# A causal convolution regrouped into 32-token blocks on two column tiles, inside a fused attention and convolution kernel

## The chip, the cores and the metric

One core of one Trainium2 chip. The metric is the device time of one execution in microseconds (us); lower is better. Each timing below is a median over executions in one series, and the kernel before was run again in every series on the same chip. Runs carry a state; verdicts and ratios use fast runs alone, and a verdict of faster or slower asks for 2%. The granted clock is the share of its full clock that TensorE had; the clock records of these traces know 1.0 and 0.5 alone, called full and half clock below. A ratio is the mean time of one kernel's fast runs over that of the other's fast runs of the same rounds, so it is not quite the ratio of the medians quoted beside it.

## The reference, cut to what matters

One layer mixes two branches by a gate per token: attention with 16 heads that share one key and value head, and a causal convolution along the sequence whose kernel K comes from a state space model. S = 2048 tokens, D = 448 channels, 256 states.

```python
g = sigmoid((x * gate_w).sum(-1))
# a: 16 query heads of 28, one key head, one value head
p = softmax((q @ k.T) * 28**-0.5);  a = (p @ v) @ wo
# b: K[d, l] = Re sum_n C[d,n] * exp(dt[d] * A[d,n] * l) * dt[d] * B[d,n]
b = causal_convolution(x, K) + x * Dskip
out = g * a + (1 - g) * b
```

The exponentials of the softmax (16 x 2048 x 2048) are the work of ScalarE, VectorE builds the tables from which TensorE makes K, and TensorE does everything else: scores (QK), attention times values (PV), the kernel generator, the convolution, the projections.

## The kernel before

The program is a list of operations with a modelled price in ns and a priority. A small scheduler, which runs when the kernel is built, orders them on each engine; the order is then fixed. The convolution works channel by channel: for a channel, T holds kernel values in a form made for matrix products, and U holds the inputs. Four channels (j) run beside each other on four column tiles, strips of 32 columns of TensorE's array that `tile_position` names.

```python
def conv(self, c):                       # a chunk of 16 channels
    for k in range(4):
        self.tload(gi)                   # T: 1 MB from device memory for 4 channels
        for m in range(1, 16, 2):
            for j in range(4):
                e.matmul(ps.v(32*j, 33-m, po + 128*k, [[1, 128]]),             # out
                         self.U.v(0, P, (m-1)*D + 4*gi + j, [[D, 33-m]]),      # weights
                         self.T.v(0, P, s*4096 + (960 - 64*m)*4 + j, [[4, 128]]),  # streamed: step of 4 elements
                         start=(m == 1), stop=(m == 15), tile_position=(0, 32*j))
            pg.op("pe", mm, 112, ..., mode="c32")       # price 112 ns for the group of four
    # ... one VectorE operation scales and flips the chunk; then ytr() transposes on TensorE and adds into O

def qk(b):                               # scores of 2 or 3 tiles of 128 x 512, then one exponential over them
    e.matmul(self.psS..., kT.v(32*h, DH+1, ...), qT..., tile_position=(32*h, 0))
    e.activation(expT..., self.psS.v(0, P, 1536*s, [[1, n]]), AF.Exp, scale=SQ)

def pv(st):                              # four heads on four column tiles, summed in psB over 16 steps
    e.matmul(self.psB.v(32*h, 32, 0, [[1, 512]]), vaug..., expT..., start=(kt == 0), stop=(kt == 15), tile_position=(0, 32*h))
```

The four channels of a T load are interleaved, element by element. Elements are bf16, so a step of 4 elements is 8 bytes.

## Time and profile before

| kernel before | value |
|---|---|
| time, median of 3 runs | 540.65 us (538.36 to 541.66) |
| span of the profiled run | 537.2 us |
| mean granted TensorE clock | 0.921 |
| busy share PE, DVE, ACT | 90%, 90%, 91% |
| exponentials: busy, idle time just before them | 470.8 us, 19.0 us |

The span is made of four parts that add up: a start, the exponentials' busy time, the gaps between them, and the tail from the last exponential to the end. With the last exponential ending at 519.5 us this is 29.7 + 470.8 + 19.0 + 17.7 = 537.2 us. "Start" here is that end less busy time less gaps. The profile lines behind it stand in the prediction.

### The profile page before, as it was taken

Reading aid. Unit: us, or ns where it says so; the run is one execution under the profiler, and the core shown is the slowest. Engines: PE = TensorE matmul, PEld = TensorE weight load, DVE = VectorE, ACT = ScalarE, POOL = GpSimd, SP = SyncE. Lnnn points to the kernel's source line nnn. Section 1 sums busy time; section 2 is a strip of 40 time slices with the busy share of each in tenths; the row PEclk is TensorE's granted clock in tenths of the full one; section 3 lists DMA queues with packets and bytes.
Section 4 is the critical chain, followed back from the end, with each engine's and each line's share of the span. In section 5 each row is a group of like instructions: output and inputs, shape, how many; then the busy total and the mean of one; then the engine's idle time right before and its main releaser. Section 6 shows DMA issues by size and latency. Waiting matters only on the chain.

```text
span 537.2 us, 18418 instructions
## 1 busy us (share of the span) xinstructions
PE 484.8 (90%) x8229; PEld 243.8 (45%) x8229; DVE 483.9 (90%) x1168; ACT 487.5 (91%) x428; POOL 4.9 (1%) x17
## 2 busy tenths in 40 slices
PE   6778888999999899999999999999999998998893
PEld 5411132553545444554545445554455543544452
DVE  4978899998999999999999999999999999999023
ACT  4599998998999999999999999999999999999960
POOL 3000000000000000000000000000000000000000
PEclk9855566997999999999999999999999999889997
DMA  8735445777798867779898896778877796697954
GB/s 232 145 79 137 138 139 207 245 285 299 249 327 297 303 230 237 253 265 345 304 337 320 262 332 238 242 260 319 309 296 267 285 393 220 176 388 254 350 188 137
DMA packets 42266, 138.16 MB, mean 257 GB/s; under 512 B 8168, under 2 KB 24476, under 8 KB 27852
## 3 DMA queue, kind: packets, MB, share of 16 engines
q1 hardware_dynamic: 40396, 135.71, 73.7%
q10 hardware_dynamic: 1792, 1.29, 0.8%
q8 instruction: 64, 1.05, 0.8%
q14 instruction: 14, 0.11, 0.1%
HBM read 133.01 MB, written 3.85 MB: 255 GB/s over the span
## 4 chain that ended last, share of the span: by engine, by line
PE 47%; ACT 36%; DVE 12%; DMA 2%; issue 1%; POOL 1%; DVEq 0%; POOLq 0%
ACT expT L977 35%; PE psS L967 13%; PE psS L853 12%; PE psB L985 8%; PE psX L792 6%; PE psX L676 2%; DMA T<-KP_scratch 2%; DVE tab L767 2%; DVE tmp L762 2%; DVE tab L759 2%; PE psS L504 1%; PE psX L877 1%; PE psX L831 1%; DVE O L883 1%; DVE tab L776 1%
## 5 line engine op out<-in xcount | busy, mean ns | idle before, releaser
L977 ACT ACTIVATE expT<-psS 128x1536 bf16<-128x1536 f32 (+1 forms) x410 | 470.8, 1254 | 19.0 <-PE psB L985 12.9
L967 PE MATMUL psS<-qT,kT 29*128 29x512 bf16 x1024 | 170.6, 412 | 29.6 <-ACT expT L977 27.2
L853 PE MATMUL psS<-T,U 128*26 128x128 bf16 (+7 forms) x3584 | 157.9, 303 | 0.6 <-DMA T<-KP_scratch 0.5
L853 PEld LDWEIGHTS psS<-T,U 128*26 128x26 bf16 (+7 forms) x3584 | 113.9, 152 | 35.3 <-issue 28.2
L985 PE MATMUL psB<-expT,vaug 128*32 128x512 bf16 x1024 | 108.8, 417 | 1.4 <-ACT gtok L643 1.3
L967 PEld LDWEIGHTS psS<-qT,kT 29*128 29x128 bf16 x1024 | 39.6, 92 | 124.4 <-ACT expT L977 92.8
L762 DVE TENSOR_TENSOR tmp<-tab,mbf 128x2048 bf16<-128x2048 bf16 (+4 forms) x140 | 78.0, 563 | 0.0
L759 DVE TENSOR_TENSOR tab<-tab,mbf 128x2048 bf16<-128x2048 bf16 (+4 forms) x140 | 77.9, 563 | 0.0
L767 DVE TENSOR_TENSOR tab<-tab,tmp 128x2048 bf16<-128x2048 bf16 (+4 forms) x140 | 77.8, 563 | 0.0
L792 PE MATMUL psX<-tab 128*32 128x96 bf16 x1792 | 54.8, 268 | 1.3 <-issue 1.2
L985 PEld LDWEIGHTS psB<-expT,vaug 128*32 128x32 bf16 x1024 | 26.6, 95 | 64.2 <-issue 60.8
L792 PEld LDWEIGHTS psX<-tab 128*32 128x32 bf16 x1792 | 41.2, 116 | 14.2 <-issue 9.0
L776 DVE TENSOR_TENSOR tab<-tab,mbf 128x2048 bf16<-128x2048 bf16 x28 | 34.0, 1216 | 0.0
L778 DVE TENSOR_TENSOR tab<-tab,mbf 128x2048 bf16<-128x2048 bf16 x28 | 34.0, 1213 | 0.0
L861 DVE TENSOR_TENSOR cst<-psS,omq 128x512 bf16<-128x512 f32 x28 | 19.0, 680 | 15.7 <-PE psS L853 15.5
L717 DVE TENSOR_TENSOR msq<-mst 128x256 f32<-128x256 f32 x63 | 26.2, 416 | 0.0
L676 PE MATMUL psX<-xT,Wq 112*128 112x512 bf16 x64 | 21.7, 436 | 0.4 <-DVE O L838 0.2
L727 DVE CAST mbf<-mst 128x256 bf16<-128x256 f32 x70 | 20.1, 288 | 0.1
L720 DVE TENSOR_TENSOR mst<-msq 128x128 f32<-128x128 f32 x70 | 19.7, 282 | 0.0
L723 DVE SCALAR_TENSOR_TENSOR mst<-mst 128x128 f32<-128x128 f32 x63 | 17.8, 283 | 0.0
L804 DVE TENSOR_REDUCE kstg<-psX 128x128 bf16<-128x256 f32 x28 | 11.7, 418 | 4.2 <-PE psX L792 4.1
L730 DVE TENSOR_SCALAR mbf<-mst 128x128 bf16<-128x128 f32 x70 | 15.3, 218 | 0.0
(112 smaller groups left out, 255.8 us busy)
## 6 DMA issues: line engine op xcount, KB each, us to landing
T<-KP_scratch SPq DMA_DIRECT2D x112, 1024.0 KB, 7.8
rdenB<-R_scratch SPq DMA_DIRECT2D x60, 64.0 KB, 3.8
U<-in_A_x_dram SPq DMA_DIRECT2D x3, 896.0 KB, 5.4
tab<-in_A_x_dram SPq DMA_DIRECT2D x4, 448.0 KB, 6.9
O<-Z_scratch SPq DMA_DIRECT2D x1, 1792.0 KB, 13.6
KP_scratch<-kstg SPq DMA_DIRECT2D x28, 64.0 KB
xT<-in_A_x_dram SPq DMA_DIRECT2D x1, 1792.0 KB, 9.2
U<-Z_scratch SPq DMA_DIRECT2D x1, 896.0 KB, 8.0
```

Source lines behind the costliest of these rows:

```text
L676: pg.op("pe", lambda e, T=T: e.matmul(px, self.Wq.v(0, DT, T * 512 + g * 128, [[1, 128]]), self.xT.v(0, DT, T * S + 512 * qc, [[1, 512]]), ...
L717: pg.op("dve", lambda e, k=k: e.tensor_tensor(msq.v(0, P, 0, [[1, 2 * BW]]) if k > 1 else msq.v(0, P, 0, [[BW, 2], [1, BW]]), src_both(k - ...
L759: pg.op("dve", lambda e, d=dst, a=src, ra=ra, w=w: e.tensor_tensor(d, a, mbf.v(0, P, ra, [[8, 16], [0, 2 * w], [1, 4]]), ALU.mult), el(n, ...
L762: pg.op("dve", lambda e, a=src, rb=rb, w=w: e.tensor_tensor(tmp.v(0, P, so, [[4 * w, 32], [1, 4 * w]]), a, mbf.v(0, P, rb, [[4, 32], [0, w ...
L767: pg.op("dve", lambda e, d=dst, t=t2: e.tensor_tensor(d, d, t, ALU.add), el(n, 1.92), rd=[("tmp", s), ("tab", s, lv + 1)], wr=[("tab", s, ...
L776: pg.op("dve", lambda e: e.tensor_tensor(ua, src, mbf.v(0, P, ra, [[8, 8], [0, 64], [1, 4]]), ALU.mult), el(2048, 1.92), rd=rk + mk, wr=[( ...
L778: pg.op("dve", lambda e: e.tensor_tensor(ub, src, mbf.v(0, P, rb, [[4, 16], [0, 32], [1, 4]]), ALU.mult), el(2048, 1.92), rd=rk + mk, wr=[ ...
L792: r = e.matmul(self.psX.v(32 * g, 32, 96 * jj, [[1, 96]]), tab.v(0, P, o + 768, [[4, 32]]), tab.v(0, P, o, [[256, 3], [4, 32]]), start=(co ...
L853: r = e.matmul(ps.v(32 * j, 33 - m, po + 128 * k, [[1, 128]]), self.U.v(0, P, (m - 1) * D + 4 * gi + j, [[D, 33 - m]]), self.T.v(0, P, s * ...
L967: r = e.matmul(self.psS.v(0, P, 1536 * s + 512 * k, [[1, 512]]), kT.v(32 * h, DH + 1, 128 * kt, [[1, 128]]), qT.v(32 * h, DH + 1, 512 * qs ...
L977: pg.op("act", lambda e: e.activation(expT.v(0, P, 512 * (i0 % 10), [[1, n]]), self.psS.v(0, P, 1536 * s, [[1, n]]), AF.Exp, scale=SQ), 75 ...
L985: r = e.matmul(self.psB.v(32 * h, 32, 0, [[1, 512]]), vaug.v(0, P, 32 * kt, [[1, 32]]), expT.v(0, P, 512 * ((4 * st + h) % 10), [[1, 512]] ...
```

## The change

The intent: each convolution matmul streams 64 columns instead of 128, T takes 112 loads of 512 KB in place of 1024 KB, and the flip of the results moves from a VectorE access pattern to two small TensorE matmuls with a reversal matrix J. The stacking over lag quarters gives the weights up to 64 columns, so two column tiles replace four. U is contiguous in time. The diff cut to its core:

```diff
-            for m in range(1, 16, 2):
-                def mm(e, k=k, m=m, s=s, gi=gi):
-                    for j in range(4):
-                        r = e.matmul(ps.v(32 * j, 33 - m, po + 128 * k, [[1, 128]]),
-                                     self.U.v(0, P, (m - 1) * D + 4 * gi + j, [[D, 33 - m]]),
-                                     self.T.v(0, P, s * 4096 + (960 - 64 * m) * 4 + j, [[4, 128]]),
-                                     start=(m == 1), stop=(m == 15), tile_position=(0, 32 * j), ...)
-                pg.op("pe", mm, 112, ..., mode="c32")
+            for k1 in range(2):
+                for mg in range(2):
+                        for m in range(8 * mg, 8 * mg + 8, 2):
+                            for par in range(2):
+                                r = e.matmul(ps.v(64 * par, 64 - m, po + 64 * pr, [[1, 64]]),
+                                             self.U.v(0, P, uo + (32 * par + e0 + pr) * UC + m, [[1, 64 - m]]),
+                                             self.T.v(0, P, s * self.TW + (448 - 32 * m) * 4 + 2 * k1 + par, [[4, 64]]),
+                                             start=(m == 0), stop=(m == 14), tile_position=(0, 64 * par), ...)
+                    pg.op("pe", mm, 118, ..., mode="c64")     # price 118 ns for the group of eight
...
+    def jpass(self, c):                  # in place of ytr(): flip and sum on PE
+            for z in range(2):
+                r = e.matmul(self.psX.v(0, P, 0, [[1, 256]]), self.J.v(0, P, P * z, [[1, P]]), self.cst..., start=(z == 0), stop=(z == 1))
...
-        sizes = [4] * 7
+        sizes = [2, 5, 7, 7, 7]          # masters in 5 blocks
```

Besides: the output projection and the skip term work in halves of 224 channels, x is kept reversed in time within blocks, U comes in 28 loads of many small pieces, and some of the scheduler's constants change.

## The prediction

> **What bounds the kernel now.** I read the page first: its engine totals and its slices.
>
> ```profile
> PE 484.8 (90%) x8229; PEld 243.8 (45%) x8229; DVE 483.9 (90%) x1168; ACT 487.5 (91%) x428; POOL 4.9 (1%) x17
> ...
> PEclk9855566997999999999999999999999999889997
> DMA  8735445777798867779898896778877796697954
> ```
>
> Three engines are near 90%, so no single share names the bound. The slices also show TensorE at half clock in slices 3 to 7 (27 to 94 us). Next the busy time by stretch (PE, PEld, DVE, ACT, POOL, clock, DMA share, GB/s):
>
> ```profile
> 100.00:450.00 350.00, 334.50 (x6192) 174.04 (x6191) 345.41 (x853) 339.65 (x297) 0.63 (x2) 0.99 0.82 291
> ...
> 500.00:520.00 20.00, 17.52 (x299) 8.90 (x298) 2.13 (x4) 19.53 (x18) 0.00 (x0) 1.00 0.90 306
> ```
>
> In the steady stretch ScalarE (the softmax exponentials) has 97%, VectorE 99%, TensorE 96%. They stop each other in turn, because each engine keeps a fixed order. VectorE starts the last instruction of its last table at 485.2 us. ScalarE ends its exponentials at about 519.5 us. Then the waits and ScalarE's timeline:
>
> ```profile
> ACT expT L977 <- PE psB L985: 12.9, 27, 1.4
> ACT expT L977 <- PE psS L967: 4.4, 10, 0.7
> ```
> ```profile
> 216.63 55.25 ACT L977 ACTIVATE expT<-psS 128x1536 bf16<-128x1536 f32 x48 [0.43 <-PE psB L985]
> ```
> ```profile
> 33.68 5.72 ACT L977 ACTIVATE expT<-psS 128x1024 bf16<-128x1024 f32 x5
> 40.53 2.36 ACT L977 ACTIVATE expT<-psS 128x1536 bf16<-128x1536 f32 x2 [1.14 <-PE psB L985]
> ```
>
> In the best stretch 48 exponentials (24 pairs of 1536 and 1024 columns) took 55.25 us, 2.29 us a pair. All 205 pairs therefore need 469 us: the floor of this program. Three exponentials (3.6 us) lie before 33.68 us, mixed with four table loads. Without gaps the last would end at 33.68 + 469 - 3.6 = 499 us. It ended at 519.5. So **about 20 us are waits of ScalarE**, and the two wait lines name TensorE for 17 of them: that is what this change can win in the middle. The end:
>
> ```profile
> 528.69 0.44 PE L831 MATMUL psX<-ident,cst 128*64 128x64 bf16 x16 [0.83 <-DVE cst L861]
> 529.33 0.42 DVE L838 TENSOR_TENSOR O<-O,psX 128x256 bf16<-128x256 bf16 x1
> 529.78 0.96 SPq L106 DMA_DIRECT2D out_dram<-O  x2
> 529.78 1.05 ACTq L106 DMA_DIRECT2D out_dram<-O  x2
> ```
>
> The last chunk of the convolution is finished after the attention, and since every chunk adds to every row of O, all four stores wait for it. From the last exponential to the end are 17.7 us.
>
> **What the Trainium skill says.** "TensorE: Matmul & The Clock Gate", Back-to-back issue gap, gives a floor of about 25 ns between matmuls of up to 64 columns; this would ruin the change. The trace disagrees for two column tiles, as shown below (16.7 ns). "SBUF — State Buffer", Specifications (TRN2), says lines are 16 bytes and want two hits each for full bandwidth. Before, U is loaded with a step of 896 bytes, T streamed with a step of 8; afterwards U has a step of 2 bytes, T still 8. The trace shows that streams are slow here, not which operand is at fault. "TensorEngine Tiling (Array Packing)", Key Properties, says that changing the tiling mode drains the engine. The trace agrees: a PV group of four 512-column matmuls (213 ns of columns at the full clock of 2.4 GHz that the first page gives) ends 0.33 us after the QK group before it, so a switch costs about 0.1 us. "DMA: Bandwidth & Descriptors", Why small descriptors are slow (HBM only), warns of small pieces, and the new loads of U have pieces of 32 to 128 bytes.
>
> **The change, part by part.** First, the convolution matmuls. Their number stays at 3584. Before: 128 columns on four column tiles. After: 64 columns on two column tiles, up to 64 weights. The nearest relative in the old kernel is the transposition at L831: 64 weights, 64 columns, two column tiles.
>
> ```profile
> 301.48 1.16 PE L853 MATMUL psS<-T,U 128*32 128x128 bf16 x32
> ...
> 304.13 0.45 PE L831 MATMUL psX<-ident,cst 128*64 128x64 bf16 x16
> ```
> ```profile
> L831 PE MATMUL psX<-ident,cst 128*64 128x64 bf16 x448 | 12.7, 198 | 2.1 <-DVE cst L861 1.7
> ```
>
> Taking one duration off a run gives the spacing: (1160 - 310)/31 = 27.4 ns before, (450 - 198)/15 = 16.7 ns for the relative. Four tiles of 128 columns at full rate would take 53 ns, 13 ns each: the old form has half the stream rate, the relative nearly all of it. If the new form goes like the relative, 3584 x (27.4 - 16.7) = 38 us less on TensorE. The transposition gives way to two matmuls of 256 columns a chunk (213 ns against 267), -1.5 us. The output projection has 256 matmuls of 224 columns on two tiles instead of 64 of 448 on one: the same columns. But the convolution now has another tiling mode than PV and the kernel generator; in the built programs' orders the mode changes 937 times instead of 884, +5 us. Sum: **about -34 us of TensorE work**, from 96% to some 88% in the middle. All of it lies beside the exponentials; its worth is only the part of the 20 us of gaps that it closes.
>
> Second, VectorE. The masters come in 5 blocks instead of 7: 52 instructions a block, 104 fewer. Successive small ones start 0.14 us apart at 128 elements and 0.20 at 256, so 0.07 us is the fixed part: -7 us. Output and skip in halves of 224 columns add 32 instructions net of the merged multiplications, +1 us. **About -6 us**; the order puts all the skip work (some 14 us) after the last table, so VectorE still has work until some 10 us before the end of the exponentials.
>
> Third, transfers. T is 112 loads of 512 KB instead of 1024: 59 of queue 1's 136 MB go, which at its 73.7% share are about 170 us of each engine. U now comes in 28 loads of 2048 small pieces. Queue 10's 1792 packets of 720 bytes on average took 0.8% of 16 engines' 537 us, 38 ns each; 57,344 pieces at that price are 136 us on each engine. The DMA share changes little. One load lands in about 2048 x 38/16 = 4.9 us plus 2; the last quarter of a group is asked for only when the chunk just before has been evacuated, but evacuations run from 105.0 to 528.0 us, 423/27 = 15.7 us apart, so it should be in time.
>
> Fourth, the start. In the order of ScalarE the two sines and their table loads now come before the first exponential, one block of about 8 us, with one table load fewer among the exponentials. The inputs of the first sine should be ready near 20 us, its second and the seed exponential by 25, so exponentials run through from about 28.5 us; the old equivalent was 33.68 - 3.6 = 30. A gain of 1.5 us, partly given back by reversed copies of x and more load issues.
>
> Fifth, the end. The order has the last convolution some seven attention steps before the end, the stores of three quarters wait for nothing late, and only the last 448 KB follow the attention. The chain from last exponential to last addition is 10.2 us now; without the convolution in between and with half-width additions 8.6. The last store alone should take 4.5 to 5 us instead of 7.4. **17.7 becomes 13.5 us.**
>
> Sum: 28.5 + 469 + gaps + 13.5. With gaps of 8 us instead of 20 the span is 519 us. The runs before lay 1.8 us (profiled run) to 3.5 us (median) above the span, so **522 us**, 3.4% faster.
>
> **Rivals.** (a) The 8-byte step halves the rate of each stream by itself, however many run: then 64 columns on two tiles cost 27 ns each, as now. For it: the generator's four tiles of 96 columns also have that step and also about half rate, and L831 has a step of 4. Against it: four streams sharing one limit explain it as well. TensorE would then carry 4 us more than before; only end, start and VectorE remain: about 535 us. (b) VectorE takes over as bound, at 99% with 6 us off: TensorE then stands at tables not ready, gaps stay near 14 us, 528 us. For it: its idle time in 100 to 450 us is only 4.6 us. Against: it finished its tables 33 us before the exponentials. (c) A late U quarter stops TensorE's fixed order, six times: at 3 us each, 535 to 540 us. For: small pieces behind T loads in one queue; against: a chunk's time in reserve. (d) Everything fits, gaps of 3 us and a quicker start: 514 us.
>
> **Range and chances.** The main path has about two thirds; (b) and (d) are variants near it, (a) and (c) have some 12% and 8%. 2% is 529.8 us. So 513 to 536 us, and chances 0.78, 0.17, 0.05.
>
> **What would show it.** Right: conv runs with 16 to 18 ns a matmul, 64 columns; ScalarE's waits for TensorE below 8 us; the last convolution before the last exponential; one store last, last exponential to end near 13.5 us. Wrong: conv spacing of 25 ns or more (a, or the page's floor); VectorE never idle while TensorE waits for tables (b); waits of TensorE for U (c); a half-clock stretch that lasts longer than before, since the lighter convolution leaves TensorE more idle.

## The result

The changed kernel is correct and **slower**: 573.67 us median (571.03 to 575.53, 4 runs) against 540.1 us (538.36 to 541.66, 4 runs), ratio 1.0619, 95% interval 1.0558 to 1.068.

The page of the changed kernel, engine totals, TensorE clock in 40 slices, and three groups (busy and mean ns, then idle time before and what ended it):

```profile
PE 511.2 (89%) x8048; PEld 253.8 (44%) x8048; DVE 489.5 (85%) x1085; ACT 492.2 (86%) x428; POOL 14.7 (3%) x15
...
PEclk9855655999977878899958999799898999978955
...
L1018 ACT ACTIVATE expT<-psS 128x1536 bf16<-128x1536 f32 (+1 forms) x410 | 475.4, 1244 | 49.2 <-PE psS L1008 25.6
...
L886 PE MATMUL psS<-T,U 128*64 128x64 bf16 (+7 forms) x3584 | 136.0, 237 | 1.6 <-issue 1.6
```

TensorE was to become lighter; its busy time grew from 484.8 to 511.2 us, in part because the same work takes longer at half clock (a score matmul 442 ns on average, 412 before). The clock now falls below full in many slices in the middle, where the kernel before had nines, and in the last three. The gaps before the exponentials grew from 19.0 to 49.2 us. The sum is 29.8 + 475.4 + 49.2 + 18.9 = 573.3 us, against 29.7 + 470.8 + 19.0 + 17.7 before: 30 of the 36 us are gaps, 5 the exponentials' own busy time, 1 the tail. The start has gained nothing. Each gap counted by the clock that the trace records at its end, 30.8 of the 49.2 us lie at full clock (11.7 before) and 18.4 at half clock (7.3 before). So two causes are to be found, and the larger part of the growth is not at half clock.

The waits (us in total, times, longest) say that ScalarE waits for TensorE, from both sides:

```profile
ACT expT L1018 <- PE psS L1008: 25.6, 49, 1.5
ACT expT L1018 <- PE psB L1026: 22.0, 37, 1.4
...
PE psS L1008 <- ACT expT L1018: 35.8, 77, 3.5
```

And yet TensorE also waits for ScalarE, 35.8 us, once for 3.5 us (before: 27.2 us, longest 1.7). The two are out of step: TensorE has stretches with too much to do and stretches with too little. TensorE's timeline has convolution runs at full clock and shows the first cause:

```profile
306.61 0.89 PE L886 MATMUL psS<-T,U 128*64 128x64 bf16 x24
...
308.74 1.85 PE L886 MATMUL psS<-T,U 128*64 128x64 bf16 x56
```

32 more matmuls take 0.96 us more, 30 ns each. The prediction had 16.7. Reckoned as the prediction did, with one duration taken off, the mean over all runs of 16 or more at full clock is 29 ns (26.8 before).

What happens in a poor stretch is seen in busy time by stretch (PE, PEld, DVE, ACT, POOL, then clock, DMA share, GB/s), cut where this trace's clock can change:

```profile
286.10:289.50 3.40, 2.31 (x24) 0.70 (x21) 3.40 (x12) 3.40 (x4) 0.00 (x0) 1.00 0.83 194
289.50:292.90 3.40, 2.30 (x16) 0.43 (x12) 3.40 (x7) 3.40 (x4) 1.35 (x2) 0.50 0.02 5
292.90:296.40 3.50, 3.50 (x16) 0.70 (x13) 2.83 (x4) 2.90 (x3) 2.98 (x1) 0.50 0.00 0
...
303.20:306.60 3.40, 3.40 (x69) 1.54 (x68) 3.07 (x11) 2.79 (x4) 0.00 (x0) 0.50 0.02 5
306.60:310.00 3.40, 3.40 (x89) 2.51 (x87) 3.27 (x8) 2.90 (x3) 0.00 (x0) 1.00 0.33 88
```

In the first stretch TensorE has 24 matmuls, is busy for 2.31 of 3.40 us, and ScalarE has no gap. In the next the clock is 0.50. It stays there for 17 us, and from the third stretch on ScalarE is busy for 2.9 of 3.5 us instead of all of it. This is the second cause, and it costs after the poor stretch, not in it.

"TensorE: Matmul & The Clock Gate", Part 1, describes a free-running window of 3413 ns after which an idle TensorE falls to half clock. Traces agree with the length: between 110 and 500 us the changed kernel's stretches at half clock are 3.4, 6.8, 10.2 or 17.1 us long. To see what sends the clock down I cut fifteen traces between 110 and 500 us at these borders. Of the stretches at full clock with TensorE busy for under 0.7 of it, 67 of 89 were followed by half clock; between 0.7 and 0.85 it was 39 of 314; at 0.85 or more, 0 of 1049. So a stretch need not be idle; some 30% of it, as the trace's modelled matmul times count it, are enough. The way back is harder: of the stretches at half clock with TensorE busy for at least 0.85 of it 100 of 234 were followed by full clock, of the 26 below that none. These are counts, not yet a cause. The experiments are the test.

The tail has the half clock too. The output projection of the last attention step, in the changed kernel's timeline:

```profile
555.05 3.20 PE L913 MATMUL psS<-Wo,onT 128*64 128x224 bf16 x32
```

The same 32 matmuls take 1.72 us at full clock in run g4_d60_start below. The convolution had ended at 542 us, and with attention alone left the clock fell at 545.5 us.

### The profile page after: what moved, and what is told of

The parts are those of the page before. It is cut to its first block, busy times and chain, and to the rows that moved or that the text cites. A ratio compares the mean times of both kernels' runs of the same rounds, so it can differ in the third digit from the quotient of the medians.

```text
span 573.3 us, 18035 instructions
## 1 busy us (share of the span) xinstructions
PE 511.2 (89%) x8048; PEld 253.8 (44%) x8048; DVE 489.5 (85%) x1085; ACT 492.2 (86%) x428; POOL 14.7 (3%) x15
## 4 chain that ended last, share of the span: by engine, by line
PE 59%; ACT 26%; DVE 12%; DMA 1%; issue 1%; SPq 0%
ACT expT L1018 25%; PE psS L886 19%; PE psS L1008 16%; PE psB L1026 10%; PE psX L826 6%; PE psX L709 2%; DMA tab<-in_A_x_dram 1%; PE psX L913 1%; PE psS L531 1%; DVE tab L793 1%; DVE tab L801 1%; DVE tmp L796 1%; PE psS L913 1%; PE psX L716 1%; DVE msq L751 1%
## 5 line engine op out<-in xcount | busy, mean ns | idle before, releaser
L1018 ACT ACTIVATE expT<-psS 128x1536 bf16<-128x1536 f32 (+1 forms) x410 | 475.4, 1244 | 49.2 <-PE psS L1008 25.6
L1008 PE MATMUL psS<-qT,kT 29*128 29x512 bf16 x1024 | 182.2, 442 | 36.8 <-ACT expT L1018 35.8
L886 PE MATMUL psS<-T,U 128*64 128x64 bf16 (+7 forms) x3584 | 136.0, 237 | 1.6 <-issue 1.6
L886 PEld LDWEIGHTS psS<-T,U 128*64 128x64 bf16 (+7 forms) x3584 | 108.1, 124 | 44.1 <-issue 42.8
L801 DVE TENSOR_TENSOR tab<-tab,tmp 128x128 bf16<-128x128 bf16 (+4 forms) x140 | 78.9, 564 | 0.8
L796 DVE TENSOR_TENSOR tmp<-tab,mbf 128x128 bf16<-128x128 bf16 (+4 forms) x140 | 78.6, 561 | 0.0
L1026 PEld LDWEIGHTS psB<-expT,vaug 128*32 128x32 bf16 x1024 | 26.8, 95 | 73.6 <-issue 68.4
L751 DVE TENSOR_TENSOR msq<-mst 128x448 f32<-128x448 f32 (+2 forms) x45 | 23.5, 522 | 0.0
L838 DVE TENSOR_REDUCE kstg<-psX 128x128 bf16<-128x256 f32 x28 | 11.7, 419 | 10.7 <-PE psX L826 10.5
L762 DVE CAST mbf<-mst 128x448 bf16<-128x448 f32 (+2 forms) x50 | 17.0, 339 | 0.1
L755 DVE TENSOR_TENSOR mst<-msq 128x224 f32<-128x224 f32 (+2 forms) x50 | 16.8, 336 | 0.0
L758 DVE SCALAR_TENSOR_TENSOR mst<-mst 128x224 f32<-128x224 f32 (+2 forms) x45 | 15.1, 336 | 0.0
L985 DVE TENSOR_TENSOR onT<-acc,rdenB 128x512 bf16<-128x512 f32 x15 | 10.2, 683 | 5.1 <-DMA rdenB<-R_scratch 5.1
## 6 DMA issues: line engine op xcount, KB each, us to landing
O<-Z_scratch SPq DMA_DIRECT2D x1, 1792.0 KB, 13.5
```

What stands on the lines that cost most here:

```text
L751: pg.op("dve", lambda e, k=k: e.tensor_tensor(msq.v(0, P, 0, [[1, 2 * BW]]) if k > 1 else msq.v(0, P, 0, [[BW, 2], [1, BW]]), src_both(k - ...
L796: pg.op("dve", lambda e, a=src, rb=rb, w=w, so=so: e.tensor_tensor(tmp.v(0, P, so, [[4 * w, 32], [1, 4 * w]]), a, mbf.v(0, P, rb, [[4, 32] ...
L801: pg.op("dve", lambda e, d=dst, t=t2: e.tensor_tensor(d, d, t, ALU.add), el(n, 1.92), rd=[("tmp", lv % 2), ("tab", s, lv + 1)], wr=[("tab" ...
L886: r = e.matmul(ps.v(64 * par, 64 - m, po + 64 * pr, [[1, 64]]), self.U.v(0, P, uo + (32 * par + e0 + pr) * UC + m, [[1, 64 - m]]), self.T. ...
L1008: r = e.matmul(self.psS.v(0, P, 1536 * s + 512 * k, [[1, 512]]), kT.v(32 * h, DH + 1, 128 * kt, [[1, 128]]), qT.v(32 * h, DH + 1, 512 * qs ...
L1018: pg.op("act", lambda e: e.activation(expT.v(0, P, 512 * (i0 % 10), [[1, n]]), self.psS.v(0, P, 1536 * s, [[1, n]]), AF.Exp, scale=SQ), 61 ...
```

## The experiments

Two theories. **Step:** the 8-byte step in T holds each stream at about half rate, so TensorE has too much work. **C (clock):** a TensorE with too little to do in a stretch loses its clock, and this costs more than the work saved. The main rival to C is **W (work):** TensorE's time is what its work is, and less work is always better. The median of the kernel before was 538.0 to 538.9 us in all series; it is not repeated in each line.

### First series: step, price, columns

**e1_price.** The scheduler believes 118 ns for eight matmuls; measured are some 8 x 30 ns.

```diff
-                    pg.op("pe", mm, 118, rd=...
+                    pg.op("pe", mm, 235, rd=...
```

> The changed kernel with one number altered: the scheduler is told 235 ns for a group of eight convolution matmuls instead of 118. (The trace of the changed kernel has 56 of them in 1.85 us, so (1850-239)/55 = 29 ns each, 235 a group.) Results stay right. Theory P (the order is wrong because the price is wrong: too much convolution between two attention steps in some places, bare stretches in others, in which TensorE idles, its clock is halved and ScalarE starves): the spacing stays at 29 ns, but ScalarE's idle time before the exponentials falls from 49 us to 20-28, half-clock time in the middle from some 60 us to below 25, and the time to 540-550 us. Rival W (the work itself is too much: 29 instead of 27 ns a matmul, more mode switches): time stays above 562 us.

Correct, 579.4 us (579.01 to 586.51, 4 runs), ratio 1.0807 (1.0727 to 1.0887). The gaps fall from 49.2 to 24.9 us and the exponentials end at 526.0 us instead of 554.4, so the wrong price did bunch the work. But the time does not fall, as rival W of this text expected: the order now puts four of the 28 chunks of the convolution after the last exponential, and its last matmul ends at 563 us. Busy time from 520 us on:

```profile
520.00:577.00 57.00, 34.03 (x625) 25.72 (x625) 12.08 (x28) 5.65 (x6) 0.00 (x0) 0.66 0.54 160
```

ScalarE has 5.65 us of work in 57. What was won in gaps is paid as a tail of 51 us: with 30 ns a matmul this order did not fit the convolution beside the attention. Whether a better order could was not tried.

**e2_step2, e3_step4.** Only the step of T changes, to 2 and 4 bytes. Their outputs are wrong, which doesn't matter for the times.

```diff
-   self.T.v(0, P, s * self.TW + (448 - 32 * m) * 4 + 2 * k1 + par, [[4, 64]]),
+   self.T.v(0, P, s * self.TW + (448 - 32 * m) * 4 + 2 * k1 + par, [[1, 64]]),   # e2; [[2, 64]] in e3
```

> The changed kernel, schedule untouched, with T streamed with a step of one element (2 bytes) instead of four (8 bytes). Results are wrong on purpose (another T is read), work and shapes are the same. Theory S (the 8-byte step halves the stream's rate, as rival a of the prediction has it): spacing of convolution matmuls falls from 29 ns to 14-17 ns, which is near the 118 ns a group that the scheduler counts with, and the time falls to 515-530 us. Theory F (each pair of weight load and matmul has a floor near 29 ns with 50 to 64 weights, whatever the step): spacing stays at 27-30 ns and the time at 570 us.

> The same with a step of two elements (4 bytes), the step that the old transposition (16.7 ns apart, two column tiles of 64) had. Wrong results on purpose. Theory S: 15-18 ns if 4 bytes are still at full rate, some value between if the rate goes with the step. Theory F: 27-30 ns.

e2: 563.87 us (563.17 to 569.55, 4 runs), ratio 1.0498 (1.0437 to 1.0559). e3: 558.55 us, one look, its state unknown. TensorE's timeline of e2, convolution runs at full clock:

```profile
300.98 0.56 PE L886 MATMUL psS<-T,U 128*64 128x64 bf16 x24
...
302.68 1.04 PE L886 MATMUL psS<-T,U 128*64 128x64 bf16 x56
```

32 more matmuls now take 0.48 us, 15 ns each instead of 30; in e3 the same runs take 0.56 and 1.05 us. So the 8-byte step of T halved the rate, and a step of 4 bytes already has all of it. Weights, U, number of streams and transfers are untouched, so it is T's step and nothing else: the step theory stands for the spacing. But 3584 x 15 ns = 54 us of TensorE's time are gone, and the time is still 25 us (e2) and 20 us (e3) above the kernel before; for e2 515 to 530 us had been expected. The clock is lower than in the changed kernel: 0.803 in e2, 0.814 in e3, against 0.845.

**e4_half.** Half the columns, the step left at 8 bytes (wrong).

```diff
-   r = e.matmul(ps.v(64 * par, 64 - m, po + 64 * pr, [[1, 64]]), ..., self.T.v(..., [[4, 64]]),
+   r = e.matmul(ps.v(64 * par, 64 - m, po + 64 * pr, [[1, 32]]), ..., self.T.v(..., [[4, 32]]),
```

> The changed kernel with 32 instead of 64 streamed columns per convolution matmul, step still 8 bytes, weights unchanged; half of the results is missing on purpose. Theory S (a slow stream): spacing falls to about half, 14-16 ns. Theory F (floor of a weight load and matmul pair): stays at 27-30 ns.

584.42 us, one look, its state unknown. TensorE's timeline at full clock:

```profile
310.09 0.56 PE L886 MATMUL psS<-T,U 128*64 128x32 bf16 x24
...
311.79 1.07 PE L886 MATMUL psS<-T,U 128*64 128x32 bf16 x56
```

32 more matmuls take 0.51 us, 16 ns each, so they follow the columns that are streamed and not a fixed cost of 25 ns or more. Each is cheaper than in the changed kernel, and the time is 11 us longer. The clock of e4's page:

```profile
PEclk9755655787956779785857898695969759955556
```

The granted clock was 0.731, the lowest of all. This is where theory C came from: the less TensorE has to do, the slower the kernel.

### Second series: is it the clock?

**f1_old_light, f2_old_step2.** The same question to the kernel before, whose order on every engine stays as it was. f1 streams half the columns, f2 all of them in steps of 2 bytes; both give wrong results.

```diff
# f1
-   r = e.matmul(ps.v(32 * j, 33 - m, po + 128 * k, [[1, 128]]), ..., self.T.v(..., [[4, 128]]),
+   r = e.matmul(ps.v(32 * j, 33 - m, po + 128 * k, [[1, 64]]), ..., self.T.v(..., [[4, 64]]),
# f2
-   self.T.v(0, P, s * 4096 + (960 - 64 * m) * 4 + j, [[4, 128]]),
+   self.T.v(0, P, s * 4096 + (960 - 64 * m) * 4 + j, [[1, 128]]),
```

> The kernel before with its own convolution streaming 64 of its 128 columns (half of every output stays wrong, on purpose; weights, waits, order and transfers are as before). About 1792 matmuls each lose some 64 columns, which at the 26.8 ns that one takes in the kernel before is about 20 us of TensorE work removed. Theory C (TensorE that is given less to do loses its clock, and everything is then slower): the time does not fall, 540 to 565 us, and the time at half clock rises from 85 us to 120 us or more. Rival W (TensorE's work is what costs, so less of it is faster): 515 to 532 us with the half-clock time about as before.

> The kernel before with its T operand read in steps of 2 bytes in place of 8 (wrong results on purpose; same matmuls, same 128 columns, four column tiles). If the 8-byte step is what holds a matmul of the old convolution at 26.8 ns, its spacing falls to 14 to 20 ns; if not (weight loads or issue hold it), it stays at 25 to 27 ns. For the time: theory C says that the work saved is given back as half clock, 535 to 560 us; rival W says 515 to 532 us.

f1: 547.43 us (546.5 to 551.48, 4 runs), ratio 1.0186 (1.0125 to 1.0246). f2: 548.31 us (544.39 to 555.64, 4 runs), ratio 1.0161 (1.0102 to 1.022); its profiled run is slow, so I use its time, and of its profile only the spacing at full clock. The page of f1:

```profile
PE 469.9 (86%) x8214; PEld 228.5 (42%) x8229; DVE 483.6 (89%) x1168; ACT 487.7 (89%) x428; POOL 4.9 (1%) x17
...
PEclk9855566997898689979968859989899899997556
...
L977 ACT ACTIVATE expT<-psS 128x1536 bf16<-128x1536 f32 (+1 forms) x410 | 470.9, 1253 | 26.5 <-PE psB L985 11.3
```

No instruction of f1 has more to do than in the kernel before, the order is the same, and TensorE is busy for 15 us less. It is 1.9% slower (under the 2% of a verdict, which is unclear, but with 1 outside the interval): gaps 26.5 us instead of 19.0, and half clock where the kernel before had full clock. The time at half clock, summed over the trace's clock records, was 193 us against 85. Rival W expected 515 to 532 us and is out. (The expected text halves the work taken away: all 3584 matmuls lose 64 columns, and their spacing fell from 26.8 to 16 ns, some 38 us.) Within one program the lower clock goes with the longer time too: the four runs of f1 took 551.48 us at a mean clock of 0.805 and 546.5 to 547.81 at 0.823 to 0.835. TensorE's timeline of f2:

```profile
302.60 0.81 PE L853 MATMUL psS<-T,U 128*32 128x128 bf16 x32
```

The same 32 matmuls took 1.16 us in the kernel before (its line is in the prediction). So the old convolution had been held by the same 8-byte step, and curing this alone makes the old kernel slower too (by 1.6%, again with 1 outside the interval).

**f3_warm, f4_pair_warm.** Dead work for TensorE: matmuls with weights of zero, added onto the sums that attention values are being added to, wherever such a group stands alone between two groups of scores. f3 has e3's T. f4 has T laid out in pairs of channels, so that the step is 4 bytes and the results are right; two transfers of half the size take the place of one.

```diff
+   if me.i in self.bare and kt < 15:
+       for h in range(4):
+           r = e.matmul(self.psB.v(32 * h, 32, 0, [[1, 512]]), self.zw.v(0, P, 0, [[1, 32]]),   # zw: zeros
+                        expT.v(0, P, 512 * ((4 * st + h) % 10), [[1, 512]]), start=False, stop=False, ...)
# f4 besides
-   self.T.v(0, P, s * self.TW + (448 - 32 * m) * 4 + 2 * k1 + par, [[4, 64]]),
+   self.T.v(0, P, s * self.TW + 1024 * k1 + 2 * (448 - 32 * m) + par, [[2, 64]]),
```

> The changed kernel with T in steps of 4 bytes (the run e3_step4, 558.55 us, with some 207 us of the span at half clock) plus dead work for TensorE alone: after each group of attention-value matmuls that stands alone between two groups of scores, four matmuls of 512 columns with weights of zero are added onto the same sums, at some 65 places. Theory C: the half-clock time falls by 50 us or more below e3_step4's 207 us, ScalarE's gaps shrink from 38.6 us, and the time falls to 520 to 548 us although TensorE has more to do. Rival W: the added work costs its own length, about 65 times 0.25 to 0.5 us, and the time rises to 565 to 590 us.

> As f3_warm, but with right results: the kernel matrix and T are laid out in pairs of channels, so that T is read in steps of 4 bytes (two transfers each of half the size in place of one, the reduction into the staging buffer in two halves). Theory C with the step theory: conv matmuls 15 to 17 ns apart, and a time within 8 us of f3_warm, 520 to 550 us, and correct. If the doubled transfers or the split reduction matter: 10 us or more above f3_warm with waits of TensorE for T or for the staging copies in the profile.

f3: 567.14 us (562.76 to 568.95, 4 runs), ratio 1.0523. f4: correct, 556.24 us (550.15 to 558.73, 4 runs, the longest slow), ratio 1.0294, above its range of 520 to 550. **f3 went against theory C**: the half-clock time stayed at 204 us (207 in e3), and 567 us lies in the range of rival W. Either C was wrong here, or 57 pieces of 0.25 us (228 matmuls, four at once) were too few and in the wrong places: the poor stretches of the cut above lack up to a quarter of 3.4 us, and isolated pieces do not fill them. Between 110 and 500 us f3's half clock did fall, from 92 us in e3 to 70; after 500 us it rose from 29 to 62, nearly all in one stretch of 68 us that began at 488 us. The next series decides.

### Third series: dead work by density

**g1_pair** is f4 without dead work, the control. **g2_d60, g3_d70, g4_d60_start** add dead work after an attention-value group when the scheduler's own times show TensorE matmuls for less than 60% (70%) of the 3.4 us around it, as many pieces as are missing, up to three. g2 and g3 begin at 95 us, g4 at the start.

```diff
+   for x in order:                                       # TensorE's order, st = modelled start
+       if x.i in self.pvs:                               # g2, g3: and st[x.i] > 95e3
+           inwin = [y for y in order if t - 1700 < st[y.i] < t + 1700]
+           have = sum(y.ns for y in inwin) + sum(215 * f for u, f in add if t - 1700 < u)
+           left = sum(1 for y in inwin if y.i in self.pvs and st[y.i] >= t)
+           f = int(round((0.6 * 3400 - have) / 215 / left))     # g3: 0.7
+           if f > 0: self.fill[x.i] = min(f, 3); add.append((t, min(f, 3)))
```

> The changed kernel with right results and T in channel pairs (steps of 4 bytes), no dead work: the control for the other three and the correct counterpart of e3_step4 (558.55 us, one look). Step theory: conv matmuls 15 to 16 ns apart, and 553 to 563 us. If the pair layout itself costs something: over 565 us. Against f4_pair_warm (556.24 us): if the 53 places of dead work there helped, this run is 3 us or more slower; if they only cost, it is faster.

> g1_pair plus 114 pieces of dead work (each four matmuls of 512 columns with zero weights, on the four column tiles at once, some 0.25 us), put only after attention-value groups around which the scheduler sees TensorE matmuls for less than 60% of 3.4 us. In all traces so far a 3.41 us stretch at full clock in which TensorE is busy for under 0.7 was followed by half clock in 45 of 52 cases, one over 0.85 in 0 of 585. Theory C: half-clock time between 110 and 500 us falls by 20 us or more against g1_pair, and the time falls by 5 to 20 us. Rival W (dead work only costs): the time rises by 5 to 30 us.

> As g2_d60 with 70%: 241 pieces, some 55 us of dead work at full clock. Theory C: still less half clock than g2_d60; the time within 8 us of g2_d60, below g1_pair. Rival W: 30 to 60 us above g1_pair.

> As g2_d60, with the dead work also in the first 95 us (in all kernels so far nearly all of 23 to 95 us is at half clock). Theory C: the stretch 25 to 95 us has at most 40 us of half clock in place of some 65, and the time is 2 to 10 us below g2_d60. Rival: at half clock the dead work takes double and keeps TensorE from the scores, the start gets longer and the time is 3 to 15 us above g2_d60.

| run | time, us (lowest, highest) | ratio (95%) | half clock, us | of it 110 to 500 us |
|---|---|---|---|---|
| g1_pair | 555.94 (554.59, 563.3), 4 runs, the longest slow | 1.0372 (1.0291, 1.0453) | 197 | 100 |
| g2_d60 | 540.88 (539.78, 541.9), 4 runs | 1.004 (0.9998, 1.0082) | 98 | 17 |
| g3_d70 | 542.14 (fast runs 540.42 to 542.76), 4 runs | 1.006 (1.0016, 1.0103) | not read | not read |
| g4_d60_start | 539.11 (537.32, 540.35), 4 runs | 1.0011 (0.9969, 1.0053) | 33 | 7 |

The four are correct. The two last columns are summed over the clock records of the profiled runs. g3's profile fell on an execution of 864.86 us and is not read for the argument. g4 lies only 1.8 us below g2, less than the 2 to 10 expected, though its half clock between 25 and 95 us fell from 66 to 20 us: where half clock stands matters, and there it cost little. The pages of g1 and of g4, clock and exponentials:

```profile
PEclk9855555799898999795967999799977996868976
...
L1019 ACT ACTIVATE expT<-psS 128x1536 bf16<-128x1536 f32 (+1 forms) x410 | 471.8, 1250 | 32.8 <-PE psS L1009 17.1
```

```profile
PEclk9959989999999989999998999999999999999997
...
L1035 ACT ACTIVATE expT<-psS 128x1536 bf16<-128x1536 f32 (+1 forms) x410 | 470.1, 1255 | 21.4 <-PE psB L1048 11.5
```

g4 has 632 matmuls more than g1, 53.6 us of them busy time, which do nothing but keep TensorE busy, and it is 17 us faster. Of g1's 32.8 us of gaps, 27.9 lay at half clock (each gap counted by the clock that the trace records at its end); in g4 it is 7.2 of 21.4. The tail falls from 18.9 to 14.7 us. Nothing else differs between the two but one small memset of the zeros, so **theory C is shown on the changed kernel with the 4-byte step**. That f3 missed because of the amount and the places fits, but is argued: g1 and f4 (61 isolated pieces) have the same time, 555.94 and 556.24 us, although f4's half clock between 110 and 500 us was 71 us against 100. g3's 218 pieces (101 in g2) changed nothing more: its fast runs have a clock of 0.919 to 0.920, those of g2 0.906 to 0.917.

In g4 11.5 of the 21.4 us of gaps are now waits for the dead work itself (L1048 is its line).

### Fourth series: do the causes add?

**h1_step8_dead** is the changed kernel, 8-byte step and all, with g4's rule. **h2_cap1** and **h3_cap1_65** are g4 with at most one piece at a place, at 60% and 65%. **h4_old_dead** is the kernel before with h2's rule.

```diff
-   self.fill[x.i] = min(f, 3); add.append((t, min(f, 3)))
+   self.fill[x.i] = min(f, 1); add.append((t, min(f, 1)))      # h2, h3, h4
```

> The changed kernel as it is (T in steps of 8 bytes) with the dead work of g4_d60_start, by the same rule (195 pieces by this kernel's own schedule). If the two causes add: half-clock time below 60 us, conv matmuls still 28 to 30 ns apart, and 552 to 562 us (573.7 less the 17 us that the dead work gave with the 4-byte step). If the 8-byte step is harmless once the clock holds: 536 to 546 us. If the clock is not what costs here: 575 us or more.

> g4_d60_start with at most one piece of dead work after an attention-value group in place of up to three: 107 pieces in place of 189. In g4_d60_start 14 exponentials waited for dead work, 11.5 us in all, the longest 2.5 us. If these waits are what stands between it and the kernel before: they fall below 4 us, half-clock time stays under 60 us, and the time is 529 to 536 us, below the kernel before. If the clock needs the full amount: half clock over 80 us and 540 us or more.

> As h2_cap1 with the threshold at 65% of 3.4 us in place of 60%: 136 pieces. Expected within 4 us of h2_cap1; below it if h2_cap1 still shows over 40 us of half clock.

> The kernel before with dead work by the rule of h2_cap1 (42 pieces by its own schedule, 21 of them in the first 80 us). Its half-clock time lies almost all before 95 us, where its exponentials have hardly a gap, so there is little to gain: expected within 1% of the kernel before, 532 to 540 us, though the half-clock time falls from 85 us. If half clock costs as such wherever it falls, it gains 8 us or more.

All four are correct. (The counts of pieces in these texts are the scheduler's; the last group of each sum carries none, so 158 ran in g4, 184 in h1, 98 in h2, 126 in h3 and 41 in h4.)

h1: 564.99 us (563.44 to 566.58, 4 runs), ratio 1.0482 (1.0418 to 1.0545), half clock 39 us. Its waits and one of its convolution runs at full clock:

```profile
ACT expT L1034 <- PE psS L1024: 19.0, 42, 1.5
ACT expT L1034 <- PE psB L1042: 13.3, 22, 1.4
ACT expT L1034 <- PE psB L1047: 9.8, 22, 1.0
```

```profile
305.55 1.85 PE L901 MATMUL psS<-T,U 128*64 128x64 bf16 x56
```

With the clock held, the 8-byte step still takes 1.85 us for 56 matmuls, and 38 of the 43.9 us of gaps lie at full clock. The time is 3 us above the range for "the causes add". Put together:

| | no dead work | dead work |
|---|---|---|
| step 8 bytes | 573.67 (the changed kernel) | 564.99 (h1) |
| step 4 bytes, pairs | 555.94 (g1) | 539.11 (g4) |

The step costs 18 us without dead work and 26 with it. The dead work gains 9 us with the long step and 17 with the short one. So the two do not simply add: the faster convolution leaves more poor stretches, and part of what it saves is lost as half clock unless something fills them.

h2: 546.53 us (540.96 to 551.68, 6 runs, two of them slow), ratio 1.0115; h3: 552.74 us (550.63 to 557.42, 6 runs), ratio 1.0269 (1.0197 to 1.0342, by the 2% unclear). The hope of 529 to 536 us failed; h2 came out in its other branch, half clock over 80 us and 540 us or more (its profiled run is slow and not read, but three of its four fast runs have a clock of 0.907 to 0.910, which makes about 100 us at half clock). h3 is 6 us above h2 and missed. In h3 the waits for the dead work are 12.8 us and not below 4, and its half clock is 140 us. One piece at a place is not enough to hold the clock. Why the 126 pieces of h3 do worse than the 98 of h2 I cannot say; h3's trace shows one stretch at half clock of 38 us from 488 us on, but no reason for it.

h4: 539.72 us (538.63 to 542.33, 6 runs), ratio 1.0022 (0.9982 to 1.0061): the same. Its half-clock time hardly fell (80 us against 85), so this run does not tell what the half clock of the first 95 us costs the kernel before. It does tell that dead work is no general gain that would make the comparison unfair.

No version beats both kernels: g4, at 539.11 us against 538.37 in its series, is the same as the kernel before.

## Why the prediction was wrong, point by point

**The failed step is "if the new form goes like the relative", in the convolution part.** The prediction took the transposition at L831 (64 columns, two column tiles, 16.7 ns) as the model of a matmul that differs from it in one thing, the step of the streamed operand: 4 bytes there, 8 here. Measured were 30 ns, so 3584 x (27.4 - 16.7) = -38 us became 3584 x (30 - 27.4) = +9 us. Its rival (a) had the mechanism; e2, e3, f2 and g1 show it, and the two explanations that the prediction left open (step, or four streams that share a limit) are told apart: four streams in f2 and two in e2 both speed up when the step shrinks. The right relative was in the profile before, the old convolution itself. It took 27.4 ns a matmul with four tiles, so 110 ns for 128 columns of one tile, 0.86 ns a column. The new one has 2 x 30 = 60 ns for 64 columns, 0.94. The rate per stream had hardly changed.

**Rival (a)'s size failed too:** it said 535 us. It counted TensorE's added work as harmless beside the exponentials. Two things were missing. The scheduler's price of 118 ns for eight matmuls was half the real one, so its order bunches work: 31 us of the changed kernel's gaps lie at full clock, and e1 with the right price has 8. And with the right price, in e1's order, the end of the convolution is late instead.

**The clock was missing from the sum.** The prediction counted TensorE's lighter load only as a gain ("from 96% to some 88% in the middle"), and named a longer half-clock stretch only as a sign of being wrong. Runs f1 (less work, 1.9% slower) and g1 against g4 (more work, 17 us faster) show that this term has the other sign. Even with the spacing as predicted, 15 ns, g1 took 555.94 us and not 522.

**Gaps of 8 us** were never reached: 21.4 in g4, 11.5 of them the price of holding the clock.

**What held.** The end: 13.5 us predicted, 14.7 in g4 and h1 once the clock holds (18.9 in the changed kernel, at half clock). The start: 28.5 predicted, 29.2 in g4, 29.8 in the changed kernel, 29.7 before, so its gain of 1.5 us was 0 to 0.5. VectorE as the bound (b) did not come: its share fell to 85%. That is the longer span, though: its busy time was to fall by 6 us and was 489.5 us, 486.4 in g4, against 483.9 before; where the 6 us went was not looked into. Changes of tiling mode on TensorE are 937 in the changed kernel's trace, as counted (886 before), and the estimate of 0.1 us for one holds: in g4 a PV group ends 0.33 us after the scores, and the groups of dead work after it, with no change of mode, follow 0.21 us apart. Late U (c) did not come: no wait for U is listed at all, and the transfers, said to change little, fell from 73.7% to

```profile
q1 hardware_dynamic: 98388, 79.69, 50.7%
```

of 16 engines' time, so the prediction's price of 38 ns for each small piece was too high: packets of 32 to 128 bytes took 9 to 15 ns on average in the changed kernel's trace. With g4's start, busy time and tail, the predicted sum is off by its gaps alone: 29.2 + 470.1 + 8 + 14.7 = 522 us of span against 519 predicted.

**What stays open:** by what measure TensorE's activity sets the clock. Busy time in 3.4 us orders the cases well, but h3 does not fit, and dead work may count otherwise than the rest. Also, the other parts of the change (VectorE's blocks, the start, the end, the scheduler's constants) were not tested one by one; all runs on the changed kernel carry them.

## What to carry to other kernels

Before a matmul form is priced after another instruction, compare the byte step of the streamed operand, and take the rate per stream and column from the old form of the same operation, if it keeps that step. In a kernel that another engine bounds, TensorE's work is not free to remove: look at the granted clock, find the stretches of some 3.4 us in which TensorE would be busy for less than about 70 to 85% (the bounds that these traces showed), and spread the remaining work over them, or the saving comes back as half clock. A scheduler's price that is off by two turns into gaps even where the sum of the work fits.

## What the Trainium skill lacked or had wrong

- "SBUF — State Buffer", Specifications (TRN2), says that two hits in a 16-byte line give full bandwidth. A step of 8 bytes in the streamed bf16 operand has two hits a line and ran at half rate: 30 ns a matmul of 64 columns on two column tiles, against 15 ns at steps of 2 and 4 bytes (changed kernel, e2, e3). All these runs have two or four streams at once; none has one alone.
- "TensorE: Matmul & The Clock Gate", Back-to-back issue gap, gives a floor of about 25 ns between matmuls, with no word on column tiles. On two column tiles the mean was 15 ns (e2, g1), and 16 ns at 32 columns with the long step (e4). (The page's part on row and column tiling does let matmuls on different tiles start closer together; the floor is not tied to it.)
- The same page, Part 1, tells of an idle window before the fall to half clock, and advises against idle gaps; of one kernel it says that short idle times between groups of matmuls made the clock swing. It gives no share of busy time for such windows: in these traces 67 of 89 windows at full clock with TensorE busy for less than 70% were followed by half clock, and none of 1049 at 85% or more. Nor has it the consequence that removing work can cost time (f1, +1.9%) and dead work gain it (g4 against g1, -17 us).
- The same page warns in a caveat that the recorded clock can be unreliable. One execution of g3, of 864.86 us, shows another trap: its trace holds no clock record at all, so the 1.0 in its result is no reading, while its scores took 660 ns a matmul on average (391 in g4).
